# Attention's pools closed right after its blocks: the rest of three expert functions' products on six PSUM banks

## The chip, the cores and the metric

The kernel runs on one core of a Trainium2 chip. The metric is device time in microseconds (us) of one execution; a kernel is run several times and the median is quoted. Two kernels are compared by the ratio of their times.

## What is computed

Three layers follow one another. The first is attention over 2 x 8 heads, with 512 local positions (a band of 32 to each side) and 32 global ones. Its output, as 1152 tokens of 512 numbers, goes through a layer of three products and a maximum, and a routed layer of eight experts ends it:

```python
x = attention(...)                                    # (1152, 512)
h = np.maximum(np.maximum(x @ w1, x @ w2), x @ w3)    # 512 -> 768
x = h @ w_out                                         # 768 -> 512
logits = x @ w_gate                                   # eight experts, capacity 288
# each token goes to the expert of its largest logit: relu(x @ w1[e]) @ w2[e], times the gate
```

w1, w2, w3 and w_out of the middle layer arrive as 64-bit floats. Only the middle layer's first line (h) lies around the change.

## The kernel before

The program is written out by hand in one order, and each engine executes its own instructions in that order. Matrix operands are held as two halves, a high and a low one, and each product is three matrix multiplications (high by high, high by low, low by high).

**The middle layer's products.** The 768 columns of h are six slices of 128, which the code calls f = 0 to 5. The tokens are four windows of 256 or 288. `moe_first(f, c0, T)` makes one group: for each of w1, w2 and w3, twelve matmuls into one PSUM bank (`ph`, line 455), so 36 matmuls and three banks' fillings to a group. Six matmuls after a bank is full (`LATE = 6`) the function `part` is issued for it: for w1 ScalarE copies the bank into the SBUF tile `hA` (line 440); for w2 and w3 VectorE takes the maximum of `hA` and the bank (line 442). After the third, ScalarE writes the high half of h (line 444) and GpSimd the low half (line 445). A bank can be filled again once its reader is done. Which bank comes next is read from the list `BANKS`, which is turned by one at each filling. At first it holds the pool `ps_mm` alone, which has three banks; the other five belong to attention.

**The order of groups.** The first three slices' twelve groups are a stream (`moe_stream`, order in `ORDER`) from which the loop over attention's blocks (`for s in range(-2, NU + 6)`) pulls a few matmuls at each place, so that TensorE has work while attention waits. Five groups (three of window 3 and one each of windows 1 and 2; four of 288 tokens and one of 256) are marked 99 and can't be pulled there. They are left to the loop `while mstream.next is not None` behind the blocks: 180 matmuls.

**The weights' conversion.** `ws` is a second stream that turns the 64-bit weights, in 24 chunks of 128 x 512 numbers, into the two halves (`split64`). `take(ws, 1)` issues its next step; seven steps make a chunk, and in the loops behind attention there is a step at every fifth matmul. To a chunk belong, in this order:

- ScalarE, line 337: the absolute value of the high words, into `a`
- VectorE, line 339 and line 342: clamping and shifting of `a` in place
- VectorE, line 345: the sign joined to `a`, into `ct`
- ScalarE, line 349: the high half, out of `ct`
- VectorE, line 352: the power of two of `ct`, into `a`; and line 354: the low word times `a`, into `b`
- GpSimd, lines 355 and 356: the low half, out of `ct` and `b`

The tile `a` is chosen when a chunk begins:

```python
b = wp.tile([P, 512], I32, tag="ca", name="ca")                                       # SBUF
a = PSA[0].tile([P, 512], F32, tag="py", name="cap").bitcast(I32) if PSA else b       # PSUM, if there is a pool
```

Before attention's pools are closed `PSA` is empty and `a` is the SBUF tile `ca`; afterwards `a` is `cap`, in one of the two banks of the pool `ps_y`. The two can be told apart by these names in the profile.

**Behind the loop.** `att.close()` gives back attention's SBUF and its five banks. New pools take them: `s2` (with the second half of h, the halves of w_out, and `hA` from here on, by `hpool[0] = s2`), `ps_x` and `ps_y` (two banks each) and `ps_m4` (one). `BANKS` becomes six entries: `ps_mm` three times, `ps_m4`, and `ps_x` twice. A small load of w_gate (line 692, on SP's queue) is issued. Then follow the slices f = 3 to 5 by the same `moe_first`, the product with w_out (`moe_second`, line 749, which takes its banks from `ps_mm`), the gate and routing, and the experts, whose weights are loaded (lines 862 and 864) once the routing has said which expert is next.

Of the kernel before, what the change touches and what calls it, by code (L numbers as in the profile page):

```python
# [50 lines left out]
def tile_block(ctx: ExitStack, tc: tile.TileContext, qk, qg, v, vo, vg, w123, w_out, w_gate, w1, w2, consts, out):  # L51
# [325 lines left out]
    def w_stream():  # L377

        todo = [("w", f, i) for f in range(NF) for i in range(3)] + [("o", f, 0) for f in range(NF)]
        raw = {}  # L380

        def load(k):
            if k < len(todo):
                kind, f, i = todo[k]
                raw[k] = dma_w(w123[f, i] if kind == "w" else w_out[f * P : (f + 1) * P], f"raw{kind}{f}{i}")

        load(0)
        yield
        load(1)
        yield  # L390
        load(2)
        yield
        old = iter(())
        for k in range(len(todo) + 1):

            new = (split64 if wide else split32)(raw.pop(k), *todo[k]) if k < len(todo) else iter(())
            next(old, None)
            yield
            next(new, None)
            yield  # L400
            next(old, None)
            load(k + 3)
            yield
            for _ in range(4):
                next(new, None)
                yield
            old = new
# [11 lines left out]
    def tick():  # L419
        for d in due:  # L420
            d[0] -= 1
        flush(0)

    def flush(n=1000):
        while due and due[0][0] <= n:
            _, fn, a = due.pop(0)
            fn(*a)


    def moe_first(f, c0, T):  # L430

        wh, wl = W[f]
        hh, hl = hT[f // NF1]
        f_ = f % NF1
        hA = hpool[0].tile([P, 288], F32, tag="hA", bufs=2, name=f"hA{f}_{c0}")
        dst = hh[:, f_, c0 : c0 + T]

        def part(i, ph):
            if i == 0:
                nc.scalar.copy(hA[:, :T], ph[:, :T])  # L440
            else:
                nc.vector.tensor_tensor(hA[:, :T], hA[:, :T], ph[:, :T], op=ALU.max)  # L442
            if i == 2:
                nc.scalar.copy(dst, hA[:, :T])  # L444
                nc.gpsimd.tensor_tensor(hl[:, f_, c0 : c0 + T], hA[:, :T], dst.bitcast(F32), op=ALU.subtract)  # L445

        for i in range(3):
            pool, tag = BANKS[0]
            BANKS.append(BANKS.pop(0))
            ph = pool.tile([P, 512], F32, tag=tag, name=f"h{f}_{c0}_{i}")  # L450
            n = 0
            for c in range(4):
                a = slice((i * 4 + c) * P, (i * 4 + c + 1) * P)
                for w_, x_ in ((wh, xh), (wh, xl), (wl, xh)):
                    nc.tensor.matmul(ph[:, :T], lhsT=w_[:, a], rhs=x_[:, c, c0 : c0 + T], start=n == 0, stop=n == 11)  # L455
                    n += 1
                    if n < 12:
                        yield
            later_on(part, i, ph)
            yield  # L460

    def take(gen, n):
        for _ in range(n):
            if next(gen, StopIteration) is StopIteration:
                return False
        return True
# [110 lines left out]
    ws = w_stream()  # L577
# [7 lines left out]
    def moe_stream():  # L585
        for g, f, at in ORDER:
            at = at if isinstance(at, tuple) else (at,) * 3
            k = 0
            yield at[0]
            for _ in moe_first(f, *(WIN1[g])):  # L590
                k += 1
                if k < 36:
                    yield at[k // 12]
# [22 lines left out]
    mstream = None  # L616
# [6 lines left out]
    for s in range(-2, NU + 6):  # L623
        live, ahead = 0 <= s < NU, 0 <= s + 2 < NU
        if s == 10:
            mstream = Stream(moe_stream())
# [44 lines left out]
            routing_start()  # L671
        if s == 30:
            nc.sync.dma_start(out.rearrange("(p i) (j c) -> p (i j) c", p=64, c=P), zero[0:64].unsqueeze(1).to_broadcast([64, NT * DM // 64 // P, P]))
    k = 0
    while mstream.next is not None:
        mstream.pull(1, 100)
        k += 1
        if mstream.next is not None and k % 5 == 0:
            take(ws, 1)
    flush()  # L680
    att.close()
    s2 = phl.enter_context(tc.tile_pool(name="s2", bufs=1))
    ps_x = ctx.enter_context(tc.tile_pool(name="ps_x", bufs=2, space=PSUM))
# [9 lines left out]

    WIN2 = [(0, 256), (256, 288), (544, 256), (800, 288)]
    k = 0
    for f in range(NF1, NF):
        for c0, n in WIN2[: 2 if f == NF - 1 else 4]:
            for _ in moe_first(f, c0, n):
                tick()
                k += 1  # L700
                if k % 5 == 0:
                    take(ws, 1)
# [647 lines left out]
```

## Time and profile before

| | |
|---|---|
| median of 3 runs (lowest, highest) | 324.5 us (323.12, 324.73) |
| profiled execution: time, span | 324.16 us, 322.4 us |
| TensorE busy (PE) | 306.5 us, 95% |
| VectorE busy (DVE) | 236.8 us, 73% |
| ScalarE busy (ACT) | 181.6 us, 56% |
| GpSimd busy (POOL) | 148.4 us, 46% |
| TensorE's granted clock | 0.994 of full speed, mean |

The span goes from the first to the last instruction of the profiled execution; 1.76 us of its time lie outside. Busy shares are means over stages that have different limits. In the timeline a matmul's row gives its start and its duration, and since matmuls are pipelined the distance between two starts is what one costs. A bracket at the end of a row tells how long the engine was idle before it and what released it. PEld is the loading of weights into TensorE, SP the engine that issues loads and stores.

### The profile page before, as it was taken

The page shows a single profiled execution, that of the slowest core. Times are in us where ns is not written, and L with a number is a line of the kernel's source. Part 1 is how long each engine was busy: PE and PEld are TensorE (multiplying, and loading weights), DVE is VectorE, ACT ScalarE, POOL GpSimd, SP SyncE. Part 2 cuts the span into 40 slices and gives each one's busy share as a digit, 9 for nine tenths or more (in the row PEclk, how much of TensorE's full clock was granted, in tenths as well). Part 3 has the DMA queues.
Part 4 walks back from the last instruction along what each step waited for, and adds up shares of the span by engine and source line. Part 5 has one row for each costly group of instructions (what it writes and reads, how often), then busy time and mean ns, then how long its engine had stood idle before and what let it go on. Part 6 is the DMA issues. An engine that isn't in the chain of part 4 may idle for free. (4 is left out here: it accounts for less than half of the span.)

```text
span 322.4 us, 8727 instructions
## 1 busy us (share of the span) xinstructions
PE 306.5 (95%) x3284; PEld 260.8 (81%) x3284; DVE 236.8 (73%) x600; ACT 181.6 (56%) x457; POOL 148.4 (46%) x164
## 2 busy tenths in 40 slices
PE   7977998999999989999999999999999999999984
PEld 2544786778999989899999999999898778888852
DVE  2699577868887999999951004756787999999871
ACT  4876988786753333444331121348331789889851
POOL 1267746677694767788672000140000448731131
PEclk9999899999999999999999999999999999999999
DMA  7999887644972323332000030588564299999920
GB/s 256 412 404 401 312 297 266 234 147 149 198 201 67 103 95 93 106 130 67 0 3 0 2 130 2 176 309 323 206 212 182 79 365 399 393 403 399 383 67 22
DMA packets 27655, 64.42 MB, mean 200 GB/s; under 512 B 3018, under 2 KB 8140, under 8 KB 27600
## 3 DMA queue, kind: packets, MB, share of 16 engines
q1 hardware_dynamic: 26304, 59.91, 53.2%
q0 software_dynamic: 1296, 3.82, 3.3%
q8 instruction: 30, 0.49, 0.6%
q14 instruction: 25, 0.20, 0.2%
HBM read 60.95 MB, written 7.27 MB: 212 GB/s over the span
## 5 line engine op out<-in xcount | busy, mean ns | idle before, releaser
L455 PE MATMUL h<-xh,wh 128*128 128x256 f32 (+1 forms) x288 | 85.2, 296 | 1.7 <-DVE hA L442 1.7
L455 PE MATMUL h<-xl,wh 128*128 128x256 f32 (+1 forms) x288 | 84.3, 293 | 0.0
L455 PE MATMUL h<-xh,wl 128*128 128x256 f32 (+1 forms) x288 | 84.1, 292 | 0.0
L455 PEld LDWEIGHTS h<-xh,wh 128*128 128x128 f32 x288 | 54.9, 191 | 3.2 <-DVE hA L442 3.0
L455 PEld LDWEIGHTS h<-xh,wl 128*128 128x128 f32 x288 | 54.7, 190 | 0.6 <-issue 0.5
L455 PEld LDWEIGHTS h<-xl,wh 128*128 128x128 f32 x288 | 54.8, 190 | 0.2
L445 POOL TENSOR_TENSOR hTl<-hA,hTh 128x256 fp32r<-128x256 f32 (+1 forms) x24 | 20.4, 850 | 55.8 <-ACT hTh L444 55.8
L239 POOL CAST xh<-xs 128x128 fp32r<-128x128 f32 x32 | 14.9, 466 | 30.7 <-ACT xs L237 30.6
L749 PE MATMUL x<-hTl,wo_h 128*128 128x256 f32 (+1 forms) x96 | 28.3, 294 | 0.0
L869 DVE TENSOR_TENSOR w2l<-rawb,w2h 128x1024 fp32r<-128x1024 f32 x23 | 27.2, 1216 | 1.4 <-ACT w2h L868 1.4
L198 ACT ACTIVATE sm<-sm,nm 128x128 f32<-128x128 f32 x64 | 25.2, 398 | 4.9 <-DVE nm L193 4.8
L749 PE MATMUL x<-hTh,wo_l 128*128 128x256 f32 (+1 forms) x96 | 27.9, 291 | 0.0
L749 PE MATMUL x<-hTh,wo_h 128*128 128x256 f32 (+1 forms) x96 | 27.8, 289 | 0.0
L193 DVE CUSTOM_DVE_ANT_0 sm<-s,mask 128x128 f32<-128x128 f32 x64 | 16.0, 286 | 15.9 <-PE s L179 9.8
L442 DVE TENSOR_TENSOR hA<-hA,h 128x256 f32<-128x256 f32 (+1 forms) x48 | 20.6, 429 | 7.5 <-PE h L455 7.1
L356 POOL TENSOR_TENSOR wl<-ct,ca 128x512 fp32r<-128x512 f32 x18 | 24.7, 1370 | 2.6 <-DVE ca L354 1.4
L952 PE MATMUL py<-w2h,hhl 128*128 128x512 f32 x96 | 25.4, 395 | 0.2 <-DVE idsall L574 0.2
L869 DVE TENSOR_TENSOR w1l<-rawb,w1h 128x1024 fp32r<-128x1024 f32 x20 | 23.7, 1216 | 1.8 <-ACT w1h L868 1.7
L355 POOL TENSOR_TENSOR ct<-ct,wh 128x512 f32<-128x512 f32 x18 | 24.5, 1363 | 0.0
L349 ACT CAST wh<-ct 128x512 fp32r<-128x512 f32 x18 | 11.1, 617 | 21.9 <-DVE ct L345 21.6
L868 ACT CAST w2h<-rawb 128x1024 fp32r<-128x1024 f32 x23 | 23.3, 1048 | 0.2 <-DMA rawb<-in_w_dram 0.2
L827 POOL DMA_INDIRECT xg<-x2d,idsall x7 | 14.9, 2123 | 16.2 <-PE xp L839 15.0
(232 smaller groups left out, 719.1 us busy)
## 6 DMA issues: line engine op xcount, KB each, us to landing
rawb<-in_w_dram SPq DMA_DIRECT2D x51, 512.0 KB
raww<-in_w_dram SPq DMA_DIRECT2D x18, 512.0 KB
rawv<-in_v_dram SPq DMA_DIRECT2D x16, 512.0 KB
qk<-in_qk_dram SPq DMA_DIRECT2D x16, 320.0 KB
rawo<-in_w_out_dram SPq DMA_DIRECT2D x6, 512.0 KB
rw<-in_w_dram SPq DMA_DIRECT2D x5, 512.0 KB
out_dram<-zero SPq DMA_DIRECT2D x1, 2176.0 KB
rawg<-in_vo_dram SPq DMA_DIRECT2D x4, 512.0 KB
```

The source lines that it names most:

```text
L193: nc.vector.tensor_tensor_reduce(sm[:, j], ps[:, j, 0:P], mk, scale=-0.125, scalar=3.0e38, op0=ALU.add, op1=ALU.min, accum_out=nm[:, j : j ...
L198: nc.scalar.activation(sm[:, j], sm[:, j], AF.Exp, bias=nm[:, j : j + 1], scale=-1.0, accum_out=ssum[:, j : j + 1])
L239: nc.gpsimd.tensor_copy(dst[0], xs)
L355: nc.gpsimd.tensor_tensor(tf, tf, hi.bitcast(F32), op=ALU.subtract)
L356: nc.gpsimd.tensor_tensor(lo, tf, b.bitcast(F32), op=ALU.add)
L442: nc.vector.tensor_tensor(hA[:, :T], hA[:, :T], ph[:, :T], op=ALU.max)
L445: nc.gpsimd.tensor_tensor(hl[:, f_, c0 : c0 + T], hA[:, :T], dst.bitcast(F32), op=ALU.subtract)
L455: nc.tensor.matmul(ph[:, :T], lhsT=w_[:, a], rhs=x_[:, c, c0 : c0 + T], start=n == 0, stop=n == 11)
L749: nc.tensor.matmul(po[:, :T], lhsT=w_[:, f, d * P : (d + 1) * P], rhs=h_[:, f_, c0 : c0 + T], start=k == 0, stop=k == 17)
L868: nc.scalar.copy(h_, raw_of(j, k))
L869: nc.vector.tensor_tensor(l_, raw_of(j, k), h_.bitcast(F32), op=ALU.subtract)
L952: nc.tensor.matmul(py[0:nt], lhsT=a[:, c, a0 : a0 + nt], rhs=w_[:, c], start=i == 0, stop=i == 23)
```

## The change

The loop that finishes the stream moves from before `att.close()` to behind the new pools, right ahead of the loop over f = 3 to 5. The flush that followed it is gone, and its counter is no longer set back before the second loop. So the five groups find six entries in `BANKS` in place of three, take `hA` from `s2`, and the chunks that begin in them find `PSA` filled.

```diff
--- before.py
+++ after.py
@@ -671,13 +671,6 @@
             routing_start()
         if s == 30:
             nc.sync.dma_start(out.rearrange("(p i) (j c) -> p (i j) c", p=64, c=P), zero[0:64].unsqueeze(1).to_broadcast([64, NT * DM // 64 // P, P]))
-    k = 0
-    while mstream.next is not None:
-        mstream.pull(1, 100)
-        k += 1
-        if mstream.next is not None and k % 5 == 0:
-            take(ws, 1)
-    flush()
     att.close()
     s2 = phl.enter_context(tc.tile_pool(name="s2", bufs=1))
     ps_x = ctx.enter_context(tc.tile_pool(name="ps_x", bufs=2, space=PSUM))
@@ -693,6 +686,11 @@
 
     WIN2 = [(0, 256), (256, 288), (544, 256), (800, 288)]
     k = 0
+    while mstream.next is not None:
+        mstream.pull(1, 100)
+        k += 1
+        if mstream.next is not None and k % 5 == 0:
+            take(ws, 1)
     for f in range(NF1, NF):
         for c0, n in WIN2[: 2 if f == NF - 1 else 4]:
             for _ in moe_first(f, c0, n):
```

## Rows read from the trace of the kernel before

**Rows 1.** Busy us of each engine by stretch, TensorE's clock, transfers' share and rate.
```profile
core 0: us, PE busy (x) PEld busy (x) DVE busy (x) ACT busy (x) POOL busy (x), PEclk, DMA share, GB/s
101.67:127.53 25.86, 24.66 (x182) 23.70 (x181) 24.34 (x35) 9.01 (x20) 16.93 (x15) 1.00 0.28 86
132.86:173.83 40.97, 40.97 (x326) 40.97 (x325) 32.76 (x59) 15.31 (x34) 30.00 (x28) 1.00 0.16 53
...
200.00:230.00 30.00, 29.65 (x249) 28.00 (x248) 21.29 (x62) 15.77 (x27) 5.11 (x5) 1.00 0.73 256
...
256.00:312.00 56.00, 56.00 (x285) 44.07 (x287) 53.62 (x57) 49.25 (x63) 24.09 (x11) 1.00 0.93 350
```

**Rows 2.** Waits of TensorE: who waited for whom, us in total, times, longest.
```profile
PE h L455 <- DVE hA L442: 1.7, 4, 0.6
```

**Rows 3.** Timeline of TensorE: starts of groups, and two of the four waits.
```profile
101.67 0.30 PE L455 MATMUL h<-xh,wh 128*128 128x288 f32 x1
...
114.90 0.40 PE L455 MATMUL h<-xh,wh 128*128 128x288 f32 x1 [0.57 <-DVE hA L442]
...
127.53 0.27 PE L455 MATMUL h<-xh,wh 128*128 128x256 f32 x1
...
129.64 0.39 PE L455 MATMUL h<-xh,wh 128*128 128x256 f32 x1 [0.53 <-DVE hA L442]
...
132.86 0.30 PE L455 MATMUL h<-xh,wh 128*128 128x288 f32 x1
...
137.60 0.28 PE L455 MATMUL h<-xh,wh 128*128 128x256 f32 x1
...
141.87 0.29 PE L455 MATMUL h<-xh,wh 128*128 128x288 f32 x1
...
173.83 0.28 PE L749 MATMUL x<-hTh,wo_h 128*128 128x256 f32 x1
```

**Rows 4.** VectorE by line and shape, 101.67 to 127.53: count, busy us, mean ns.
```profile
L345 DVE SCALAR_TENSOR_TENSOR ct<-raww,ca 128x512 int32<-128x512 int32 x5 | 6.8, 1363 | 0.1
L342 DVE TENSOR_SCALAR ca<-ca 128x512 int32<-128x512 int32 x5 | 6.5, 1302 | 0.1
L339 DVE TENSOR_SCALAR ca<-ca 128x512 f32<-128x512 f32 x5 | 3.5, 695 | 1.2 <-ACT ca L337 1.2
L354 DVE SCALAR_TENSOR_TENSOR ca<-raww,ca 128x512 f32<-128x512 uint32 x5 | 3.5, 694 | 0.2
L442 DVE TENSOR_TENSOR hA<-hA,h 128x288 f32<-128x288 f32 x6 | 2.7, 442 | 0.0
L352 DVE TENSOR_SCALAR ca<-ct 128x512 int32<-128x512 int32 x5 | 2.1, 415 | 0.0
```

**Rows 5.** The same view of VectorE, 132.86 to 166.
```profile
L342 DVE TENSOR_SCALAR cap<-cap 128x512 int32<-128x512 int32 x8 | 5.6, 698 | 0.2
L339 DVE TENSOR_SCALAR cap<-cap 128x512 f32<-128x512 f32 x8 | 5.6, 695 | 1.3 <-ACT cap L337 1.3
L352 DVE TENSOR_SCALAR cap<-ct 128x512 int32<-128x512 int32 x8 | 5.5, 689 | 0.1
L354 DVE SCALAR_TENSOR_TENSOR ca<-rawo,cap 128x512 f32<-128x512 uint32 x6 | 4.1, 683 | 0.1
L345 DVE SCALAR_TENSOR_TENSOR ct<-rawo,cap 128x512 int32<-128x512 int32 x6 | 4.1, 682 | 0.5 <-POOL ct L355 0.5
```

**Rows 6.** Timeline of ScalarE: first steps of two successive chunks.
```profile
144.06 0.63 ACT L337 ACTIVATE cap<-rawo 128x512 f32<-128x512 f32 x1
...
148.04 0.65 ACT L337 ACTIVATE cap<-rawo 128x512 f32<-128x512 f32 x1
```

**Rows 7.** Timeline of VectorE: attention's last instruction, and the last maximum ahead of `moe_second`.
```profile
100.20 0.23 DVE L317 TENSOR_TENSOR xl<-gpd,xh 64x64 fp32r<-64x64 f32 x1 [0.28 <-ACT xh L316]
...
174.03 0.46 DVE L442 TENSOR_TENSOR hA<-hA,h 128x288 f32<-128x288 f32 x1 [1.06 <-PE h L455]
```

**Rows 8.** Waits of SP's queue: who waited for whom, us in total, times, longest.
```profile
SPq L1232 <- DVE order L1224: 14.8, 1, 14.8
```

## Prediction

> **What bounds the kernel now.** I read first the busy time by stretch, for the stretch that the moved loop fills and for those behind it [rows 1]. The five leftover groups run from 101.67 us, where the first starts, to 127.53, where f = 3 starts [rows 3]. In these 25.86 us TensorE is busy for 24.66 and VectorE for 24.34 [rows 1]: two engines are nearly full, and the question is which of them makes the other wait. From 132.86 to 173.83, the rest of f = 3 to 5, TensorE is busy for all of 40.97 us; there it alone is the limit.
>
> Next the waits of TensorE: four times in the whole run a product's first matmul waits for a maximum of line 442, 1.7 us of idle time in all [rows 2]. That maximum is what gives a bank back. The timeline puts them at 114.90, twice between that and 127.53, and at 129.64 [rows 3]. All four lie in the leftover groups and in the first group of f = 3, which still finds the three banks full of work that VectorE hasn't got to. So VectorE is behind, and three banks are too few to cover it.
>
> Idle time understates what such a wait costs, since a pipelined engine also refills. So I compare whole groups. A group of 256 without a wait takes 141.87 - 137.60 = 4.27 us [rows 3]. The full stretch of 40.97 us holds four such groups and five of 288, so one of 288 takes (40.97 - 4 x 4.27) / 5 = 4.78 us [rows 1, 3].
>
> Why VectorE is behind is in its rows by shape [rows 4]. A chunk costs it 695 + 1302 + 1363 + 415 + 694 = 4469 ns while `a` lies in SBUF, and there are five chunks. With two maxima of 442 ns a round of it needs 5.35 us by these means; rows overlap a little, and 25.86 / 5 = 5.17 us is what a round takes. TensorE has matmuls for 35/36 of a group in a round, 4.65 us for 288 tokens and 4.15 for 256. VectorE is the slower one by some half a microsecond a round.
>
> **The change part by part.**
>
> *Six banks.* The groups from 101.67 on may run six fillings ahead of VectorE in place of three. Three more fillings are a whole group, over 4 us. At half a microsecond a round, five rounds put VectorE about 2.5 us further behind, which fits into that. By this part alone the four waits go.
>
> *The chunks' `a` in PSUM.* The five chunks that begin in the stretch take `cap`. The price is in the rows of the chunks that already do: 695 + 698 + 682 + 689 + 683 = 3447 ns [rows 5], 1.02 us less than in SBUF. What gains is line 342 (1302 to 698) and line 345 (1363 to 682); line 352 loses (415 to 689). Two successive chunks there start 148.04 - 144.06 = 3.98 us apart [rows 6], two maxima included. That is below 4.15, so VectorE keeps up, and three banks would nearly do. So there are two reasons for the same waits to go, and either suffices; they are counted once.
>
> The Trainium skill (VectorE: DVE Perf Modes, section "Why PSUM operands drop a tier") says that an operand in PSUM takes the double rate from a one-source operation on 32-bit data, which speaks against this part. Line 352 agrees with it (415 to 689 ns), line 342 does not (1302 to 698 ns). By the Trainium skill's page alone each of the three one-source steps would lose what line 352 loses, 0.27 us, and the five chunks 15 x 0.27 = 4.1 us of VectorE; by the rows they gain 5.1.
>
> *The gain.* From 101.67 to 132.86 there are 31.19 us with four groups of 288 and two of 256, which without waits need 4 x 4.78 + 2 x 4.27 = 27.66. The excess is 3.53 us, and I take all of it. Bounds: the idle time alone, 1.7 us [rows 2], from below, and 3.53 from above, since TensorE can't run closer than in the full stretch. I take the upper one because both parts remove the cause.
>
> *`hA` from `s2`.* Its first writer, ScalarE, may have to wait for attention's last user of that memory. Attention's last instruction ends at 100.20 + 0.23 us [rows 7], and the first bank of the leftover groups is full only a third of a group after 101.67. Cost nothing; without that cover ScalarE's copies, and the conversion queued behind them, would be late by the difference. The same holds for the first use of attention's banks, a whole group later.
>
> *The lost flush and the counter.* The last maximum of the leftover groups is issued six matmuls into f = 3, under 1 us later (six times 4.27/36 is 0.71). It is hidden by the spare banks. The counter: 180 is a multiple of five, the step at 180 was and is left out, so the conversion's steps fall on the same matmuls. Cost nothing.
>
> *The turn of the list.* The leftover groups fill 15 banks, an odd multiple of three, so the last group ahead of `moe_second` now ends on the three of `ps_mm`, which `moe_second` uses too. Its third product needs the bank that the last maximum reads, at 174.03 + 0.46 us, and starts 36 matmuls after 173.83 [rows 3, 7], 4.27 us later. Cost nothing; without that distance 0.66 us.
>
> *The load of w_gate* moves ahead of five weight loads on SP's queue. It waits for nothing of the moved loop, and its data are used by the gate, behind `moe_second`. Cost nothing.
>
> *Downstream.* From 132.86 to 173.83 TensorE is full, from 200 to 230 it is busy for 29.65 of 30 us, so what it gains by 132.86 it still has at the experts. There SP waits 14.8 us for the list of experts (`order`) before it may load on [rows 8], and that list comes out of a chain behind TensorE's last logits. So the experts' loads, which keep the transfers at a share of 0.93 from 256 to 312 [rows 1], start earlier by the same 3.53 us.
>
> **Sum.** The profiled execution took 324.16 us, 322.4 of it span. 324.16 - 3.53 = 320.6. The median of the runs is 324.5, 0.34 above it, so a median of 320.6 to 321.0; I say 320.8.
>
> **The rivals.**
>
> *Part of the waits stays* (chance 0.12). Places: the chunk under way when the loop begins still has `a` in SBUF, and the order of the queues might hold VectorE behind for other reasons, such as the wait for line 337 (1.2 us in the stretch [rows 4]). Then only the idle time itself comes back: 324.5 - 1.7 = 322.8. Against it: the same wait is in the full stretch too (1.3 us [rows 5]) and TensorE doesn't feel it.
>
> *Nothing arrives at the end* (0.10). The share of 0.93 and 350 GB/s [rows 1] say that transfers are the limit of the last stage; if their start hung on something other than TensorE, the end would stay at 324.5. Against it stands SP's wait for `order` [rows 8], a price that only an earlier TensorE lowers.
>
> *Slower: VectorE's steps in PSUM cost more here than in the later stretch* (0.06). The one-source steps would have to lose on top of their present price, as line 352 does: 3 x 0.27 = 0.82 us a chunk, 4.1 over five; with VectorE setting the pace, 328.6 us. The point from which it decides is a round above the present 5.17 us. Against it: the eight chunks of [rows 5] stand beside the same matmuls and the same GpSimd work, and their mean is 3447 ns.
>
> The Trainium skill (VectorE: DVE Perf Modes, "Why PSUM operands drop a tier") would lead here, if its rule were all that acts.
>
> **How the numbers follow.** The forecast has 0.72, its own range being 319.6 to 321.8: below, the fastest run before, 323.12, less 3.53; above, the median less 2.7, halfway between the bounds of the gain. The whole range must leave out no more than 0.2: the partial case at 322.8 with 0.4 of scatter is taken in, the other two (0.16) are not, so 319.6 to 323.2. A change under 0.5% (1.6 us) is about what a measurement of this kernel can't tell from none. Faster: 0.72 + 0.12 less 0.02 for a partial case that falls under the bound, 0.82. Same: 0.10 + 0.02. Slower: 0.06.
>
> **What would show it.** Right: no wait of a product for line 442 between 100 and 135 us; groups 4.27 and 4.78 us apart; the five chunks under the name `cap`, lines 342 and 345 near 0.69 us; `moe_second` starting near 170.3; SP's experts' loads behind `order` some 3.5 us earlier; a span near 318.9. Wrong: waits for line 442 that remain, line 345 still above 1 us, ScalarE's first copy into `hA` waiting for attention, or a `moe_second` that is early and an end that isn't.

## The result, and the profile after

The changed kernel takes 321.21 us (median of 7 runs, 319.54 to 322.26) where the kernel before took 324.5 (median of 7, 323.12 to 325.52). The ratio is 0.9903, 95% interval 0.9874 to 0.9932: faster by 1.0%, with 1.1% forecast (320.8 us). Run again on another occasion it gave 0.9883 (0.9848 to 0.9917).

The profiled execution has a span of 319.7 us. The view of the busy time by stretch, in the columns of [rows 1], is cut at the starts of the same groups:

```profile
102.66:126.11 23.45, 23.45 (x183) 23.45 (x182) 21.46 (x38) 9.27 (x20) 17.63 (x16) 1.00 0.36 113
126.11:130.41 4.30, 4.30 (x39) 4.30 (x37) 3.52 (x7) 1.81 (x4) 3.03 (x3) 1.00 0.25 78
130.41:171.38 40.97, 40.97 (x326) 40.97 (x325) 31.48 (x56) 15.41 (x33) 27.60 (x26) 1.00 0.14 45
```

The timeline of TensorE has these starts, which answer to 101.67, 127.53, 132.86 and 173.83 of [rows 3]:

```profile
102.66 0.30 PE L455 MATMUL h<-xh,wh 128*128 128x288 f32 x1
...
126.11 0.27 PE L455 MATMUL h<-xh,wh 128*128 128x256 f32 x1
...
130.41 0.30 PE L455 MATMUL h<-xh,wh 128*128 128x288 f32 x1
...
171.38 0.28 PE L747 MATMUL x<-hTh,wo_h 128*128 128x256 f32 x1
```

The reader is to see three things. The five leftover groups take 23.45 us in place of 25.86, and the first group of f = 3 takes 4.30 in place of 5.33: 27.75 us in place of 31.19, a gain of 3.44. TensorE is busy for every microsecond of these stretches; its waits hold no row for line 442 any more, where [rows 2] had four. And what follows, from 130.41 to 171.38, is 40.97 us long as before, to the hundredth.

The waits of the weight loader, which the prediction did not read, also held line 442 in the kernel before. There are six of them and not four, and they come nearer to the gain than TensorE's idle time of 1.7 us does; in the changed kernel none is left:

```profile
PEld h L455 <- DVE hA L442: 3.0, 6, 0.8
```

VectorE by line and shape, 101.67 to 127.53, answers to [rows 4]:

```profile
L342 DVE TENSOR_SCALAR cap<-cap 128x512 int32<-128x512 int32 x5 | 3.5, 697 | 0.1
L339 DVE TENSOR_SCALAR cap<-cap 128x512 f32<-128x512 f32 x5 | 3.5, 694 | 0.5 <-ACT cap L337 0.5
L354 DVE SCALAR_TENSOR_TENSOR ca<-raww,cap 128x512 f32<-128x512 uint32 x5 | 3.4, 687 | 0.2
L352 DVE TENSOR_SCALAR cap<-ct 128x512 int32<-128x512 int32 x5 | 3.4, 686 | 0.0
L345 DVE SCALAR_TENSOR_TENSOR ct<-raww,cap 128x512 int32<-128x512 int32 x5 | 3.4, 683 | 0.2
```

The five chunks that begin in the leftover groups bear the name `cap` (the one under way when the loop begins still has `ca`, and TensorE doesn't feel it), and a chunk costs 697 + 694 + 687 + 686 + 683 = 3447 ns, against 4469 before. SP's wait for the list of experts is as long as in [rows 8], so the stage behind it has only moved:

```profile
SPq L1230 <- DVE order L1222: 14.9, 1, 14.9
```

From the second group of f = 3 to the end of the span there are 322.4 - 132.86 = 189.54 us before and 319.7 - 130.41 = 189.29 after. The gain of 3.44 us arrives whole. The two spans differ by 2.7 and not by 3.44 + 0.25, because in this execution the leftover groups began 0.99 us later, ahead of anything that the change touches (last section).

### The profile page after: what moved, and what is told of

Same layout as the page of the kernel before. It is cut to its first block, busy times and chain, and to the rows that moved or that the text cites. A ratio compares the mean times of both kernels' runs of the same rounds, so it can differ in the third digit from the quotient of the medians.

```text
span 319.7 us, 8726 instructions
## 1 busy us (share of the span) xinstructions
PE 306.5 (96%) x3284; PEld 261.8 (82%) x3284; DVE 231.6 (72%) x600; ACT 182.3 (57%) x457; POOL 145.7 (46%) x164
## 5 line engine op out<-in xcount | busy, mean ns | idle before, releaser
L445 POOL TENSOR_TENSOR hTl<-hA,hTh 128x256 fp32r<-128x256 f32 (+1 forms) x24 | 19.1, 797 | 54.8 <-ACT hTh L444 54.8
L355 POOL TENSOR_TENSOR ct<-ct,wh 128x512 f32<-128x512 f32 x18 | 23.6, 1311 | 0.0
L444 ACT CAST hTh<-hA 128x256 fp32r<-128x256 f32 (+1 forms) x24 | 10.0, 418 | 20.8 <-DVE hA L442 20.8
```

The lines of the kernel that those rows point to most:

```text
L355: nc.gpsimd.tensor_tensor(tf, tf, hi.bitcast(F32), op=ALU.subtract)
```

## The experiments

The change has two parts that could each take the waits away, more banks and a cheaper conversion; it also moves things that were costed at nothing. Theory: VectorE is late, and either part covers or removes that. Rivals: only one of the two counts, or the move itself does. Unless a kernel says otherwise, its edits stand on the changed kernel.

**Neither part.** The loop is moved, and banks and PSUM come after it.

```diff
-    BANKS[:] = [(ps_mm, "mm")] * 3 + [(ps_m4, "mm"), (ps_x, "px"), (ps_x, "px")]
-    PSA.append(ps_y)
...
             take(ws, 1)
+    BANKS[:] = [(ps_mm, "mm")] * 3 + [(ps_m4, "mm"), (ps_x, "px"), (ps_x, "px")]
+    PSA.append(ps_y)
     for f in range(NF1, NF):
```

> The loop is moved as in the change, but the list of banks keeps ps_mm's three and the conversion keeps SBUF until the loop is over; hA from s2, the lost flush, the counter and the early load of w_gate stay as in the change. If banks or PSUM are the cause (my theory): as before the change, ratio to it 0.998 to 1.002, four or so waits for line 442, 31.2 us from the first leftover group to the second group of f = 3. If the move itself (hA in other memory, no flush, an earlier load) brings something: waits fewer, ratio under 0.996.

Measured: 324.04 us, ratio to the kernel before 0.9995 (0.9976 to 1.0013). The starts in the timeline of TensorE:

```profile
101.11 0.30 PE L455 MATMUL h<-xh,wh 128*128 128x288 f32 x1
...
127.02 0.28 PE L455 MATMUL h<-xh,wh 128*128 128x256 f32 x1
...
132.36 0.30 PE L455 MATMUL h<-xh,wh 128*128 128x288 f32 x1
```

That is 31.25 us against 31.19, with four waits for line 442. So `hA` in other memory, the missing flush, the counter and the earlier load of w_gate cost nothing and bring nothing.

**Six banks alone.** Of the edit above only the line with `PSA` is moved.

> Six banks in the leftover groups, the conversion's a in SBUF there. My theory, that three more fillings cover VectorE's lateness of half a microsecond a round: no wait for line 442, the whole 3.5 us, ratio 0.989 to 0.991, VectorE's round still near 5.2 to 5.4 us and its last maximum of the leftover groups some 2.5 us later behind its product than in the changed kernel. Rival, that only the cheaper conversion matters: waits come back once the six are used up, ratio 0.995 to 1.0.

Measured: 321.55 us, ratio 0.9902 (0.9865 to 0.994), no wait for line 442. The starts in the timeline of TensorE, then VectorE by line and shape between 101.67 and 127.53, then VectorE's timeline: the last maximum ahead of the leftover groups, line 342 in two rounds that lie four apart, and the last maximum of the leftover groups:

```profile
103.95 0.30 PE L455 MATMUL h<-xh,wh 128*128 128x288 f32 x1
...
127.40 0.27 PE L455 MATMUL h<-xh,wh 128*128 128x256 f32 x1
...
131.70 0.30 PE L455 MATMUL h<-xh,wh 128*128 128x288 f32 x1
```
```profile
L345 DVE SCALAR_TENSOR_TENSOR ct<-raww,ca 128x512 int32<-128x512 int32 x5 | 6.8, 1368 | 0.1
L342 DVE TENSOR_SCALAR ca<-ca 128x512 int32<-128x512 int32 x5 | 6.5, 1301 | 0.1
```
```profile
105.78 0.41 DVE L442 TENSOR_TENSOR hA<-hA,h 128x256 f32<-128x256 f32 x1
...
108.50 1.12 DVE L342 TENSOR_SCALAR ca<-ca 128x512 int32<-128x512 int32 x1
...
130.18 1.40 DVE L342 TENSOR_SCALAR ca<-ca 128x512 int32<-128x512 int32 x1
...
133.21 0.44 DVE L442 TENSOR_TENSOR hA<-hA,h 128x288 f32<-128x288 f32 x1
```

27.75 us again, the same as in the changed kernel, although the conversion is as dear as before. VectorE is late all the time: its last maximum of the leftover groups starts 133.21 - 127.40 = 5.8 us after TensorE has gone on to f = 3. In the kernel before it was 3.3 us (the first row below, against 127.53 in [rows 3]), and in the changed kernel 0.2 (the second, against 126.11):

```profile
130.83 0.44 DVE L442 TENSOR_TENSOR hA<-hA,h 128x288 f32<-128x288 f32 x1
```
```profile
126.31 0.46 DVE L442 TENSOR_TENSOR hA<-hA,h 128x288 f32<-128x288 f32 x1 [0.48 <-PE h L455]
```

Here the expectation is missed: the last maximum is 5.6 us later than in the changed kernel, not 2.5. When the leftover groups began VectorE was 105.78 - 103.95 = 1.8 us late, so it fell back by another 4.0 us. Its round is longer than I had it: four rounds, from one start of line 342 to the next, take (130.18 - 108.50) / 4 = 5.42 us each, where TensorE needs 4.15 to 4.65. Six banks hold that, but not by much. The last maximum ends at 133.65, and the bank that it reads is wanted again five fillings after 127.40, at about 134.9 (an estimate: 131.70 and two thirds of a group of 4.78 us).

**The conversion in PSUM alone.** Only the line with `BANKS` is moved.

> Three banks in the leftover groups, the conversion's a in PSUM there. My theory: a round of VectorE takes 4.0 us, less than the 4.15 to 4.65 us of TensorE, so VectorE is never late by more than the banks cover; no wait or under 0.3 us of them, ratio 0.989 to 0.992. Rival, that only the number of banks matters: the waits stay, ratio 0.996 to 1.0.

Measured: 320.0 us, ratio 0.9881 (0.9851 to 0.9911), no wait for line 442. Starts in the timeline of TensorE:

```profile
100.95 0.30 PE L455 MATMUL h<-xh,wh 128*128 128x288 f32 x1
...
124.40 0.27 PE L455 MATMUL h<-xh,wh 128*128 128x256 f32 x1
...
128.70 0.30 PE L455 MATMUL h<-xh,wh 128*128 128x288 f32 x1
```

27.75 us for the third time, with three banks. Either part alone is the whole change; that the median lies 1.2 us under the changed kernel's is not its doing, as the intervals overlap and the stretch is equally long.

**Four banks.** How many banks are enough? The conversion's `a` is in SBUF, and the loop has `[(ps_mm, "mm")] * 3 + [(ps_m4, "mm")]`; the list of six comes behind the loop, as in the first experiment.

> Four banks in the leftover groups, the conversion's a in SBUF. Each filling of 288 tokens is 1.59 us that VectorE may be later. If VectorE's lateness grows to the 3.5 us that three banks make TensorE wait, four leave 3.5 - 1.6 = 1.9 us of waits, ratio 0.994 to 0.996. Rival, that any spare bank breaks the jam: no wait, ratio 0.990. Rival, that the banks don't matter: 3.5 us of waits, ratio 1.0.

Measured: 324.54 us, ratio 1.0015 (0.9994 to 1.0035): nothing gained, and the first rival's "any spare bank" is as wrong as my 1.9 us. The waits are fewer inside the leftover groups and come back at the start of f = 3. Rows of TensorE's timeline, then two of ScalarE's:

```profile
101.12 0.30 PE L455 MATMUL h<-xh,wh 128*128 128x288 f32 x1
...
126.84 0.39 PE L455 MATMUL h<-xh,wh 128*128 128x256 f32 x1 [1.32 <-ACT hA L440]
...
129.13 0.39 PE L455 MATMUL h<-xh,wh 128*128 128x256 f32 x1 [0.60 <-DVE hA L442]
...
132.35 0.30 PE L455 MATMUL h<-xh,wh 128*128 128x288 f32 x1
```
```profile
124.95 0.62 ACT L349 CAST wh<-ct 128x512 fp32r<-128x512 f32 x1 [3.68 <-DVE ct L345]
...
126.41 0.37 ACT L440 COPY hA<-h 128x288 f32<-128x288 f32 x1
```

From the first leftover group to the second group of f = 3 it is 31.23 us, against 31.19. The first of the two waits ends with ScalarE's copy of a bank, but that copy stands behind a conversion step that waited 3.68 us for VectorE's line 345; here too VectorE is what is late. The list of six is new there and begins at `ps_mm`, whose three banks had been filled just before. My reading is that the fourth bank lets VectorE be later, and the restart presents the bill at once. Two runs test this reading.

**The list turned, in the kernel before.** The new list begins on attention's three banks; nothing else is changed.

```diff
-    BANKS[:] = [(ps_mm, "mm")] * 3 + [(ps_m4, "mm"), (ps_x, "px"), (ps_x, "px")]
+    BANKS[:] = [(ps_m4, "mm"), (ps_x, "px"), (ps_x, "px")] + [(ps_mm, "mm")] * 3
```

> The kernel before, with the list of six turned by three: f = 3 begins on the three banks that attention gave back and comes to ps_mm afterwards. The leftover groups are untouched. If the waits at the start of f = 3 come only from finding ps_mm full again: the first group of f = 3 takes 4.3 us in place of 5.33, three waits for line 442 in place of four, the leftover groups still 25.9 us; 1.05 us gained, ratio 0.996 to 0.998. Rival, VectorE's lateness is passed on whatever bank is next: the wait only moves to a later group, ratio 1.0.

Measured: 322.9 us, ratio 0.9965 (0.994 to 0.999), three waits for line 442. Starts in the timeline of TensorE:

```profile
101.92 0.30 PE L455 MATMUL h<-xh,wh 128*128 128x288 f32 x1
...
127.80 0.28 PE L455 MATMUL h<-xh,wh 128*128 128x256 f32 x1
...
132.12 0.30 PE L455 MATMUL h<-xh,wh 128*128 128x288 f32 x1
```

The leftover groups take 25.88 us as before, the first group of f = 3 takes 4.32 in place of 5.33: the 1.0 us there belongs to the restart.

**Four banks, and the list turned.** The edits of the last two runs together.

> Four banks in the leftover groups, a in SBUF, and the list of six turned as in the run before. With four banks and the list not turned, one wait of 0.5 us was left inside the leftover groups, and 2.5 to 3 us came at the start of f = 3, where the fresh list begins at ps_mm again. If that restart is what gave the gain back: one wait of 0.5 us, f = 3 without a wait, 3.0 us gained, ratio 0.990 to 0.992. Rival, four banks are too few in any case: the wait moves behind f = 3's first group, ratio above 0.996.

Measured: 321.61 us, ratio 0.9914 (0.9886 to 0.9942). In the timeline of TensorE:

```profile
102.20 0.30 PE L455 MATMUL h<-xh,wh 128*128 128x288 f32 x1
...
124.72 0.40 PE L455 MATMUL h<-xh,wh 128*128 128x288 f32 x1 [0.34 <-DVE hA L442]
...
126.42 0.37 PE L455 MATMUL h<-xh,wh 128*128 128x256 f32 x1
...
130.82 0.30 PE L455 MATMUL h<-xh,wh 128*128 128x288 f32 x1
```

28.62 us, 0.87 more than without any wait and 2.57 less than before; one wait is left that four banks don't cover. Of the 2.57 us, 1.0 is the turned list's. Against the run with the list turned and three banks, which takes 25.88 + 4.32 = 30.20 us, the fourth bank gains 1.58, about one filling. So one bank more is worth 1.6 us or nothing, by where the list goes on.

**Less of the conversion in the stretch.** The kernel before, three banks, `a` in SBUF, with `k % 7 == 0` for `k % 5 == 0` in the leftover loop: the same work, spread thinner. A single execution comes first, then the timing on another occasion.

> The kernel before, with a step of the conversion at every seventh matmul in place of every fifth in the leftover groups; the ten steps that this leaves over come later, after f = 5. Three banks, a in SBUF. My theory (VectorE's work to a round is what is too much): a round of 49 matmuls has 5.9 to 6.5 us for 5.7 us of VectorE; no wait for line 442 in the leftover groups, which take 23.4 us in place of 25.9. What comes of the end is open, since the steps left over come ahead of the product with w_out. Rival, three banks are too few whatever VectorE does: the waits stay.

> The kernel before with a conversion step at every seventh matmul in the leftover groups, this time timed. Its one look left no wait there and gave 320.4 us. If TensorE without a gap is all that there is to be had: the same gain as the change, ratio 0.988 to 0.992, and no difference from the changed kernel on the same chip beyond 0.3%. Rival, the steps left over cost something ahead of the product with w_out: ratio above 0.993.

Measured: 320.38 us in the one execution; timed, 321.08 us, ratio 0.9885 (0.9847 to 0.9923), beside the changed kernel's 320.55 and 0.9883 (0.9848 to 0.9917) on the same occasion.

> The changed kernel once more, on the chip of the run before: ratio 0.988 to 0.992.

The starts in TensorE's timeline of the first execution are 27.75 us apart once more, and no wait for line 442 is left:

```profile
101.74 0.30 PE L455 MATMUL h<-xh,wh 128*128 128x288 f32 x1
...
129.49 0.30 PE L455 MATMUL h<-xh,wh 128*128 128x288 f32 x1
```

So what is too much is VectorE's work within these rounds. The ten steps that I took to be left over behind f = 5 cost nothing that can be seen: the stretch from f = 3 on had the room. VectorE's last conversion step starts at 167.99 us there, ahead of the product with w_out at 170.46.

**Why lines 342 and 345 are long in SBUF.** The kernel before without GpSimd's subtraction of line 355, so the low half of the middle layer's weights is another number; there is one execution (320.66 us), and only the stretch is read.

```diff
-        nc.gpsimd.tensor_tensor(tf, tf, hi.bitcast(F32), op=ALU.subtract)
```

> The kernel before without GpSimd's subtraction of line 355, so the low half of the middle layer's weights is another number and GpSimd has half the conversion's work. Theory, lines 342 and 345 are long in SBUF because they stand behind a GpSimd instruction on the same memory side: in the leftover groups one of them falls to what it costs alone (0.41 us for line 342, 0.69 for line 345), the two together from 2.67 us to 1.9 or less, and with them the waits for line 442 go. Rival, they are long by their own form or operands: 1.30 and 1.36 us as before.

Measured: VectorE by line and shape between 101.67 and 127.53, then one pair in the timelines of GpSimd and VectorE (behind the line left out the numbering has moved up by one, so the old line 356 is 355), and line 342 at a time when GpSimd is idle:

```profile
L342 DVE TENSOR_SCALAR ca<-ca 128x512 int32<-128x512 int32 x5 | 6.0, 1204 | 0.1
...
L345 DVE SCALAR_TENSOR_TENSOR ct<-raww,ca 128x512 int32<-128x512 int32 x6 | 4.1, 685 | 0.1
```
```profile
118.06 1.48 POOL L355 TENSOR_TENSOR wl<-ct,ca 128x512 fp32r<-128x512 f32 x1
```
```profile
118.42 1.40 DVE L342 TENSOR_SCALAR ca<-ca 128x512 int32<-128x512 int32 x1
```
```profile
100.83 0.43 DVE L342 TENSOR_SCALAR ca<-ca 128x512 int32<-128x512 int32 x1
```

One of the two falls, from 1363 to 685 ns; the other stays at a mean of 1204 and ends, at 119.82, 0.28 us behind GpSimd's instruction, at 119.54. Where GpSimd does nothing, from 100.51 to 103.16, the same step takes 0.43 us. No wait for the maxima (line 442, here 441) is left. Each of the two long steps was standing behind one of GpSimd's two. In PSUM neither does, with GpSimd's work as it was: 697 and 683 ns.

The Trainium skill (SBUF — State Buffer, section "SBUF: two separate sides") says that VectorE and GpSimd share one pair of SBUF ports, which a VectorE instruction in a two-port mode, or with two SBUF inputs, and a GpSimd instruction that reads SBUF hold against each other for a whole instruction. The rows agree: line 342, with 0.43 us in SBUF when GpSimd is idle and 0.69 us in PSUM, is of the first kind in SBUF; line 345, with both inputs in SBUF, is of the second; and with `a` in PSUM they are neither.

## Why the prediction was right, step by step

- *What bounds the stretch.* Right: VectorE was late and three banks did not cover it. Thinning VectorE's work out with three banks takes every wait away, and so do six banks with VectorE as late as 5.8 us.
- *How late VectorE is.* Mis-sized, though the sum did not rest on it. The forecast had half a microsecond a round, 2.5 us over the stretch; with six banks alone it was 4.0 us, from a round of 5.42 us. The 5.17 us came of dividing 25.86 by five, but at 35 matmuls a round the 180 matmuls are 5.14 rounds, and the stretch ends while VectorE is still behind. That six banks were enough was closer than forecast: the estimate above leaves 1.2 us.
- *Two reasons, either suffices.* Right, and shown: each part alone gives the 27.75 us of both.
- *The price of a chunk in PSUM.* Forecast 3447 ns from [rows 5], measured 3447 ns.
- *The Trainium skill's rule on PSUM operands* (VectorE: DVE Perf Modes, "Why PSUM operands drop a tier"). Line 352 paid for it, 415 to 686 ns, in the changed kernel as in [rows 5]; the time did not, since the two lines that stood behind GpSimd gained more.
- *The gain.* Forecast 3.53 us, measured 3.44 in the stretch. I was right to take the excess of whole groups and not the 1.7 us of [rows 2]: those rows hold half of the loss, and four of the six waits that the weight loader's row counts (3.0 us).
- *The parts costed at nothing.* Right, by the run with neither part (0.9995). That run lacks the turn of the list ahead of `moe_second`; for it stand the 40.97 us and the end that comes no later.
- *Downstream.* Right: 189.54 us before and 189.29 after from the second group of f = 3 on.
- *What the prediction left unsaid.* It named the first group of f = 3 as a place of excess and put it down to VectorE's being late. It is also the list's restart: 1.0 us of the 3.53 came back by turning the list alone. The sum was not touched, since the change takes both away; for four banks, where I expected 1.9 us of waits, all 3.5 stayed.
- *The rivals.* Neither a part that stays, nor an end that stands still, nor dearer steps in PSUM showed.

## What to carry to other kernels

A wait for a PSUM bank says only that its reader is late: look at what else that engine does in a round before adding banks, since a cheaper or thinner-spread round can give the same time without a bank. When a list of buffers is exchanged in mid-run, begin the new one at the buffers that have been free longest; in this kernel that was 1.0 us by itself, and without it a fourth bank was worth nothing. Cost waits of TensorE from group to group: the idle time beside the matmuls was half of the loss, and the weight loader's waits, 3.0 of 3.44 us, came nearer.

## What was not expected of the hardware

The leftover groups begin between 100.95 and 103.95 us in the kernels shown here, though, the run without line 355 apart, nothing ahead of them differs. The view by stretch shows TensorE's granted clock between 20 and 40 us, first of the kernel before and then of the changed one:

```profile
20.00:40.00 20.00, 16.93 (x346) 10.68 (x348) 16.15 (x58) 15.34 (x64) 16.03 (x24) 0.91 0.96 366
```
```profile
20.00:40.00 20.00, 17.03 (x325) 10.80 (x324) 15.92 (x53) 14.87 (x60) 15.52 (x22) 0.83 0.91 343
```

Full speed is 2.4 GHz; a mean of 0.91 or 0.83 says that the clock was at its lower level, 1.2 GHz, for a part of the 20 us. TensorE was busy for only some 17 of the 20 us there, with attention's small products. The executions with 0.83 begin the leftover groups at 102.66 (the change) and 103.95 (six banks alone), those with 0.91 between 100.95 and 102.20; the one with four banks had 1.00 and begins them at 101.12, no sooner than some with 0.91. So the clock is a part of it only. VectorE's timeline has these rows for the same work, first of the kernel before and then of the changed one:

```profile
34.23 0.66 DVE L354 SCALAR_TENSOR_TENSOR ca<-raww,ca 128x512 f32<-128x512 uint32 x1
...
50.50 0.65 DVE L342 TENSOR_SCALAR ca<-ca 128x512 int32<-128x512 int32 x1
...
58.20 0.29 DVE L307 TENSOR_TENSOR dg<-gpv,gss 128x128 f32<-128x128 f32 x1 [0.70 <-PE gpv L305]
```
```profile
34.91 0.66 DVE L354 SCALAR_TENSOR_TENSOR ca<-raww,ca 128x512 f32<-128x512 uint32 x1
...
52.39 0.66 DVE L342 TENSOR_SCALAR ca<-ca 128x512 int32<-128x512 int32 x1
...
59.09 0.29 DVE L307 TENSOR_TENSOR dg<-gpv,gss 128x128 f32<-128x128 f32 x1 [0.60 <-PE gpv L305]
```

The changed kernel is 0.68 us behind at the first, 1.89 at the second and 0.89 at the third. About 1.2 us go with the lower clock; the 0.68 before and the 1.0 that comes back after have other causes, which were not traced. What sets how long the clock stays low in an execution was not tried either. In all the leftover groups' start scatters by 3 us, as much as the change is worth, so the comparisons above are made from group to group and not from span to span.
